# The second expert layer by seven quarter products, with one w2 place in use and a landing place

## The chip, the cores and the metric

The kernel runs on one core of a Trainium2 chip. The metric is device time in microseconds (us) of one execution. TensorE is called PE, VectorE DVE, ScalarE ACT, GpSimd POOL, and SyncE, which only issues transfers here, SP.

## What is computed

A chunked attention gives a row of 512 numbers for each of 4608 tokens. A router picks one of eight experts for each token, and the expert is a layer of two matrices:

```python
logits = xn @ en.T / tau
expert_idx = np.argmax(logits, axis=1)
for e in range(E):
    mask = expert_idx == e
    h = np.maximum(x[mask] @ w1[e], 0.0)          # 512 -> 1024
    out[mask] = gate_w[mask, None] * (h @ w2[e])  # 1024 -> 512
```

All numbers are fp32. The gate is one over the sum of the exponentials of the token's logits.

## The kernel before

A first stage of about 200 us does the attention and the routing, tile by tile, and writes each token's row into a list in memory (`spots`), sorted by expert. A second stage of about 450 us works off this list in steps. A step takes two groups of 64 tokens; group s=0 goes through the experts from the first upwards, group s=1 from the last downwards, so each side s keeps one expert's weights for many steps. The steps are numbered j; the first NE=4 belong to experts 0 and 7 and begin inside the attention, steps 4 to 35 follow (32 steps), and the last ones run under conditions.

The order of instructions is written out by hand: each engine executes its own in the order in which the program states them, and the pools place the waits. The loop at L1141 works in iteration j on hidden layer j+1 and on the result of step j, and prepares step n=j+2.

- **Hidden layer** (`hidden_fast`, L330). x is 128 tokens by 512. Each of the two matrices is cut in quarters (B11, B12, B21, B22), and seven products of sums of quarters replace eight plain ones. Sums of w1 (T1, T2, T4 in `sums_sb`, T3 in the place of B12) are made by `add_up` (L285) when an expert comes; sums of x (s1 to s4) by `add_x` (L309) on DVE in each step. A product is eight matmuls of 32 tokens by 256 columns in four column tiles of PE. ACT copies the first product from PSUM to U, DVE adds the others (`add`, L376) to c11, c12, c22 and U, ACT applies relu (L363, two instructions for each quarter), DVE transposes (L370) into hT. The tile C has four places, for U, c11, c12 and c22, and h two.
- **Result** (`result`, L406). 32 matmuls of 32 tokens by 512 columns over the eight parts of hT, directly with w2, into one of two PSUM banks, in turns. ACT scales with the gate (L423), and one indirect store on POOL (L430) writes whole rows of 512.
- **Weights.** w1 has one place in use and one landing place, `next_w1`. `load_behind` (L188) has SP load the next expert under a condition. `take_next` (L297) is a conditional block on DVE and ACT for each side: where the step begins a new expert, ACT copies three quarters (L303) and DVE makes the four sums (L293). w2 has two whole places per side, which the steps use in turns; `load_w2` (L183) loads each under the condition `fresh`.
- **Gates** (`gate_parts`, L219). POOL raises the sum of squares to the power -1/2 through `halves`, DVE subtracts and scales the logits, ACT takes the exponential with its sum, DVE takes the reciprocal. One gate per partition.
- **Inputs of a step.** `load_x` loads x into one of three places and the logits into `spot`; `turn_xb` (L200) transposes x with DVE. The loop calls them three and two steps ahead.

In the loop of before, in the order of an iteration: the hidden layer j+1 (with the gates, the transposes of x and the sums of x for n in between, `turn_next`, and `take_next` for n after the last product, `swap_next`), then the result of j, then the loads.

Of the kernel before, what the change touches and what calls it, by code (L numbers as in the profile page):

```python
# [25 lines left out]
def kernel(  # L26
# [34 lines left out]
    LONE = NE + 1  # L61

    def buf_of(j):
        return 0 if j < LONE else (j - LONE + 1) % 2

    def next_of(j):

        return j + 1 if j + 1 < LONE else j + 2

# [22 lines left out]
    half = halves[:, 0:1]  # L94
    w1_sb = [keep.tile([P, KD, F], FP32, name=f"w1_{s}") for s in range(2)]
    w2_sb = [[keep.tile([P, KF, D], FP32, name=f"w2_{s}0")] for s in range(2)]
    xin_sb = [keep.tile([P, D], FP32, name=f"xin{i}") for i in range(XBUF)]
    SPOTS = 8
# [8 lines left out]
    fresh = keep.tile([P, NST], I32, name="fresh")  # L107
# [13 lines left out]
    bp = ctx.enter_context(tc.tile_pool(name="blk", bufs=2))  # L121

# [24 lines left out]
    def load_rows(j, rows):  # L147
# [3 lines left out]
        for s in range(2):  # L151
            for b in range(G // Q if s < len(rows) else 0):
                c = s * (G // Q) + b
                ins.append(
                    nc.sync.dma_start(
                        out=xin[j][:, c * P : c * P + P],
                        in_=rows[s][Q * b : Q * b + Q, 0:D].rearrange("i (r d) -> r i d", d=P),
                    )
                )
            ins.append(  # L160
                nc.sync.dma_start(out=spot[G * s : G * s + G, j % SPOTS], in_=rows[s % len(rows)][:, D:RW])
            )
# [20 lines left out]
    def load_w2(j):  # L183
        for s in range(2):
            at = of_step(s, j)
            load_when(w2_sb[s][buf_of(j)], w2_rows, eblk[at], fresh[at])

    def load_behind(j):  # L188

        c = LEAST - 2 - j  # L190
        for s in range(2):
            at = (slice(G * s, G * s + 1), slice(c, c + 1))
            load_when(next_w1[s], w1_rows, after[at], more_e[at])

    def load_late(j):
        for s in range(2 if j != LEAST else 1):
            at = of_step(s, j)
            load_when(next_w1[s], w1_rows, eblk[at], swap[at])

    def turn_xb(j):  # L200
        t = xin.pop(j)
        xT = bp.tile([P, KD, P], FP32, tag="xbT", name="xbT")
# [16 lines left out]
    def gate_parts(j):  # L219
        lg = spot[:, j % SPOTS, 0:E]  # L220
# [3 lines left out]
        last = "_last" if j == LEAST - 1 else ""  # L224
        gate = bp.tile([P, 1], FP32, tag="gate" + last, name="gate", bufs=5)
        nc.gpsimd.tensor_tensor(rn, spot[:, j % SPOTS, SQ : SQ + 1], half, ALU.pow)  # L226
# [12 lines left out]
    def hidden_part(j, s, b, w1, pool, tag, ps=None):  # L239
# [4 lines left out]
        if b == 0:  # L244
# [3 lines left out]
            if s == 0:  # L248
                d["hT"] = bp.tile([P, KF, P], FP32, tag="hT", name="hT", bufs=2)
# [12 lines left out]
        if b == G // Q - 1:  # L262
            h = bp.tile([P, G // Q, KF * Q], FP32, tag="h", name="h", bufs=1)
# [21 lines left out]
    def add_up(s, w1, which):  # L285
        for o, a, b in (
# [3 lines left out]
            ("T4", "T2", "B21"),  # L290
        ):
            if o in which:
                nc.vector.tensor_tensor(  # L293
                    block(s, o), block(s, a, w1), block(s, b, w1), ALU.subtract
                )

    def take_next(j):  # L297

        for s in range(2):
            f = number(swap[of_step(s, j)], 1, ENG.DVE, ENG.Activation)  # L300
            with tc.If(f > 0):  # L301
                for m in ("B11", "B21", "B22"):
                    nc.scalar.copy(block(s, m), block(s, m, next_w1))  # L303
                add_up(s, next_w1, ("T1", "T2", "T3", "T4"))
# [4 lines left out]
    def add_x(j):  # L309

        x = quarters(mo[j]["xT"])
        S = late_p.tile([P, 3, KD // 2, 2, Q], FP32, tag="S", name="S", bufs=2)
        s1, s2, s3, s4 = x[:, 0, 1], S[:, 0], S[:, 1], S[:, 2]
        for o, a, b, op in (
# [5 lines left out]
            nc.vector.tensor_tensor(o, a, b, op)  # L320
        mo[j]["S"] = (s1, s2, s3, s4)

# [7 lines left out]
    def hidden_fast(j, ps_h, gate, turn_next, swap_next):  # L330
# [21 lines left out]


        last = "_last" if j == LEAST - 1 else ""
        hT = bp.tile([P, KF, P], FP32, tag="hT" + last, name="hT", bufs=1 if last else 2)
        d["hT"] = hT
        C = late_p.tile([P, 4, W2], FP32, tag="C", name="C")
        U, c11, c12, c22 = (C[:, i] for i in range(4))
        h = [late_p.tile([P, 2, W2], FP32, tag=f"h{b}", name=f"h{b}") for b in range(2)]

        def relu(b, v, x):
            for s in range(2):
                nc.scalar.activation(  # L363
                    h[b][G * v : G * v + G, s].rearrange("p (k i) -> p k i", i=Q),
# [4 lines left out]
        def turn(b):  # L369
            nc.vector.transpose(  # L370
                hT.rearrange("p k (s b i) -> p b s k i", b=2, i=Q)[:, b],
                h[b].rearrange("p s (k i) -> p s k i", i=Q),
# [8 lines left out]
        next(gate, None)  # L381
        p2 = product(x[:, 1, 0], "B21")
        add(c11, U, p2)
        next(gate, None)
        relu(0, 0, c11)
        turn_next()
        p3 = product(s4, "B22")
        p5 = product(s1, "T1")
        p6 = product(s2, "T2")
        add(U, U, p6)  # L390
        add(c12, U, p5)
        add(c12, c12, p3)
        relu(0, 1, c12)
# [4 lines left out]
        add(c22, U, p5)  # L398
        relu(1, 1, c22)
        p4 = product(x[:, 1, 1], "T4")  # L400
        swap_next()
        add(U, U, p4, ALU.subtract)
        relu(1, 0, U)
        turn(0)
        turn(1)

    def result(j, ps_y):
# [4 lines left out]
        for c in range(KF):  # L412
            for r in range(P // Q):
# [4 lines left out]
                    rhs=w2_sb[s][buf_of(j)][:, c, d0 : d0 + w],  # L418
# [3 lines left out]
        y = bp.tile([P, D], FP32, tag="y", name="y", bufs=1)  # L422
        nc.scalar.activation(y[:, 0:w], ps[:, 0:w], AF.Copy, scale=gate_of.pop(j))  # L423
        to, at, bound = out, spot[:, j % SPOTS, TOK : TOK + 1].bitcast(I32), N - 1
        if one_group:
# [3 lines left out]
            to, at, bound = out.rearrange("n (s d) -> (n s) d", s=2), at2, 2 * N - 1  # L429
        ins = nc.gpsimd.indirect_dma_start(  # L430
            out=to,
            out_offset=bass.IndirectOffsetOnAxis(ap=at, axis=0),
            in_=y[:, 0:w],
# [14 lines left out]
    with (  # L448
# [12 lines left out]
        xr = one.tile([P, NX, W], FP32, name="xr")  # L461
        blank = one.tile([P, W], FP32, name="blank")
        pad(qk_p, 40, "pad_qk")
# [47 lines left out]
        def constant_parts():  # L511
# [46 lines left out]
            nc.gpsimd.tensor_scalar(in_g, second, -float(G), at, ALU.mult, ALU.add)  # L558
            nc.gpsimd.tensor_scalar(e_p, second, float(R), None, ALU.mult)
# [333 lines left out]
        def places(d0, d1):  # L893
# [37 lines left out]
            if d0 == 0:  # L931
                first_e = e_of[:, j1 - 1 : j1]
                nc.vector.tensor_scalar(fresh[:, j1 - 1 : j1], first_e, e_0, None, ne)
                nc.vector.memset(fresh[:, j0 : j1 - 1], 1)
# [4 lines left out]
            else:  # L939
# [4 lines left out]
                    fresh[:, j0:j1], e_of[:, j0:j1], e_of[:, j0 + 2 : j1 + 2], ne  # L944
                )
                nc.vector.tensor_tensor(
# [7 lines left out]
                nc.vector.tensor_tensor(fresh[:, j0:j1], fresh[:, j0:j1], used, ALU.mult)  # L954
# [84 lines left out]
        for t in range(-3, NT + 3):  # L1039
# [31 lines left out]
            if t == NT - 6:  # L1071
                load_first([w[0] for w in w2_sb], w2_rows)
# [38 lines left out]
    pad(late_p, 40, "pad_late")  # L1111
    for s in range(2):
        w2_sb[s].append(late_p.tile([P, KF, D], FP32, name=f"w2_{s}1"))

    next_w1 = [late_p.tile([P, KD, F], FP32, name=f"next_w1_{s}") for s in range(2)]
    sums_sb = [late_p.tile([P, 3, KD // 2, F // 2], FP32, name=f"sums_{s}") for s in range(2)]

    load_x(NE)
    load_x(NE + 1)
    load_w2(LONE)  # L1120

    with (
# [17 lines left out]
        first_parts()  # L1140
        for j in range(LEAST - 1):  # L1141
            n = j + 2

            def turn_next():
                if n < LEAST:
                    turn_xb(n)
                    if n + XBUF < NJ:
                        load_x(n + XBUF)
                    add_x(n)

            def swap_next():
                if NE <= n < LEAST:
# [6 lines left out]
            elif j == 1:  # L1159
                turn_next()  # L1160
                add_up(1, None, TS)
                hidden_plain(2, w1_sb, lambda s: add_up(s, None, ("T3",)))
            else:
                gate = gate_parts(n) if n < LEAST else iter(())
                hidden_fast(j + 1, ps_h, gate, turn_next, swap_next)

            result(j, ps_y)
            if NE <= next_of(j) < NJ:
                load_w2(next_of(j))
            if NE - 1 <= n < LEAST - 1:  # L1170
                load_behind(n)
            elif n == LEAST - 1:
                load_late(LEAST)

        steps = number(n_steps, NST, ENG.PE, ENG.DVE, ENG.Activation, ENG.Pool, ENG.SP)
# [3 lines left out]
        def before_last():  # L1179
            result(LEAST - 1, ps_y)  # L1180
            load_w2(LEAST + 1)

        def step_alone(j, between=None):
            turn_xb(j)
# [4 lines left out]
            if j + 1 < NJ:  # L1189
                load_late(j + 1)  # L1190
# [3 lines left out]
            if j + 2 < NJ:  # L1194
                load_w2(j + 2)
# [51 lines left out]
```

## Time and profile before

| what | value |
|---|---|
| runs | median 673.86 us of 3 (670.34 to 679.64) |
| the profiled execution | 673.45 us, span 671.7 us |
| PE, DVE, ACT, POOL busy | 623.1, 420.9, 353.9, 180.8 us |
| a step without a switch of experts | 12.91 us |
| PE busy from 240 to 600 us | 352 of 360 us |
| expert switches in the loop (copies of L303: 18, three each) | 6 |
| DMA in such a step | 14 to 17% of the engines' time |

How it is read: a row of a group gives line, engine, operation, out<-in, shape and count, then busy time and mean time of one in ns, then how long the engine was idle just before and what ended most of that. In a timeline a row gives start and duration in us, and in brackets the idle time before it. "DVEq" and "ACTq" are the sequencers of the engines: branches, register loads and waits. PE takes an fp32 matmul as two records, and four column tiles run side by side, so the sum of the records' durations is more than PE's busy time.

### The profile page before, as it was taken

To read this page: it belongs to the slowest core of one execution; us is meant where nothing else is said; L and a number is where in the kernel's file an instruction comes from. 1 tells how busy PE (TensorE), PEld (TensorE's weight loads), DVE (VectorE), ACT (ScalarE), POOL (GpSimd) and SP (SyncE) were. 2 spreads that over 40 slices of the span, in tenths; PEclk is the share of its full clock that TensorE was granted. 3 is DMA by queue.
4 is the path that set the end of the run, shared out by engine and by line. 5 is a ranking of instruction groups with operands and counts; after the bars stand their busy time and mean duration, and the time that the engine had idled before them with its cause. 6 is when DMAs were issued, how large, how long until landed. Compare 5 with 4: busy or idle time off the path is not lost. (4 is left out here: it accounts for less than half of the span.)

```text
span 671.7 us, 24786 instructions
## 1 busy us (share of the span) xinstructions
PE 623.1 (93%) x9744; PEld 336.0 (50%) x9744; DVE 420.9 (63%) x1140; ACT 353.9 (53%) x671; POOL 180.8 (27%) x274
## 2 busy tenths in 40 slices
PE   4979988998898989999999999999999999999993
PEld 4868877785443434455334444344444444444431
DVE  2958878885597546547675566757655666565430
ACT  4747766674114444555466546555555566555530
POOL 6739887843330100011000100011001000100101
PEclk9989999998998999999999999999999999999998
DMA  9999999979718711113785111776821115411111
GB/s 248 239 247 253 254 285 274 276 251 368 304 55 297 286 45 34 51 34 129 294 313 181 50 42 42 284 279 238 309 79 57 39 46 170 164 41 35 50 31 35
DMA packets 94686, 112.66 MB, mean 168 GB/s; under 512 B 52460, under 2 KB 72684, under 8 KB 94552
## 3 DMA queue, kind: packets, MB, share of 16 engines
q1 hardware_dynamic: 82824, 72.84, 33.9%
q0 software_dynamic: 11696, 38.04, 17.3%
q8 instruction: 81, 1.33, 0.8%
q14 instruction: 53, 0.43, 0.2%
q10 hardware_dynamic: 32, 0.02, 0.0%
HBM read 334.71 MB, written 22.69 MB: 532 GB/s over the span
## 5 line engine op out<-in xcount | busy, mean ns | idle before, releaser
L415 PE MATMUL y_ps<-w,hT 128*32 128x512 f32 (+1 forms) x2368 | 274.0, 587 | 2.6 <-DVE C L376 2.1
L363 ACT ACTIVATE h<-C 64x256 f32<-64x256 f32 x264 | 179.3, 679 | 108.9 <-DVE C L376 82.4
L415 PEld LDWEIGHTS y_ps<-w,hT 128*32 128x32 f32 x2368 | 85.9, 110 | 161.3 <-issue 146.9
L430 POOL DMA_INDIRECT out_dram<-y,spot x36 | 36.9, 1025 | 412.8 <-ACT C L379 200.1
L376 DVE TENSOR_TENSOR C<-C,h 128x256 f32<-128x256 f32 x231 | 96.1, 416 | 48.3 <-DVEq L301 41.2
L344 PE MATMUL h<-w,S 128*32 128x256 f32 x1056 | 101.4, 382 | 1.8 <-DVE w L293 1.8
L344 PE MATMUL h<-sums,xbT 128*32 128x256 f32 x1056 | 101.0, 383 | 0.0
L344 PE MATMUL h<-w,xbT 128*32 128x256 f32 x1056 | 80.7, 380 | 7.4 <-ACTq L301 5.8
L370 DVE STREAM_TRANSPOSE hT<-h 128x512 f32<-128x512 f32 x66 | 46.7, 708 | 44.7 <-ACT h L363 44.6
L344 PEld LDWEIGHTS h<-w,xbT 128*32 128x32 f32 x1056 | 40.1, 110 | 44.7 <-ACTq L301 14.5
L344 PEld LDWEIGHTS h<-w,S 128*32 128x32 f32 x1056 | 48.0, 110 | 25.4 <-DVE w L293 1.5
L344 PEld LDWEIGHTS h<-sums,xbT 128*32 128x32 f32 x1056 | 48.2, 111 | 22.9 <-issue 0.9
L233 ACT ACTIVATE sh<-sh 128x8 f32<-128x8 f32 x37 | 7.7, 209 | 87.7 <-DVE sh L231 87.7
L229 DVE TENSOR_SCALAR rn<-rn 128x1 f32<-128x1 f32 x37 | 5.7, 153 | 73.3 <-POOL rn L226 73.3
L344 PE MATMUL h<-sums,S 128*32 128x256 f32 x528 | 49.9, 379 | 0.0
L815 POOL DMA_INDIRECT spots<-xr,dest x36 | 37.4, 1038 | 30.6 <-DVE dest L780 10.1
L205 DVE STREAM_TRANSPOSE xbT<-xin 128x256 f32<-128x256 f32 x73 | 44.5, 645 | 0.5 <-DVE hT L370 0.5
L423 ACT ACTIVATE y<-y_ps,gate 128x512 f32<-128x512 f32 (+1 forms) x37 | 25.2, 682 | 29.4 <-issue 13.8
L697 ACT COPY xT<-tr 128x512 f32<-128x512 f32 x36 | 21.1, 586 | 31.3 <-PE tr L695 31.3
L587 POOL DMA_DIRECT2D kx<-in_k_dram x36 | 32.0, 893 | 18.0 <-PE tr L610 17.6
L587 POOL DMA_DIRECT2D qx<-in_q_dram x40 | 34.4, 866 | 1.4 <-PE tr L610 0.7
L695 PE MATMUL tr<-ident,xr 128*128 128x128 f32 x144 | 23.1, 282 | 9.7 <-DVE xr L677 7.2
(200 smaller groups left out, 777.5 us busy)
## 6 DMA issues: line engine op xcount, KB each, us to landing
w<-in_moe_w_dram SPq DMA_DIRECT2D x74, 2048.0 KB
next_w<-in_moe_w_dram SPq DMA_DIRECT2D x67, 2048.0 KB
xin<-spots SPq DMA_DIRECT2D x158, 64.0 KB
qx<-in_q_dram POOLq DMA_DIRECT2D x32, 256.0 KB
v<-in_v_dram SPq DMA_DIRECT2D x56, 144.0 KB
kx<-in_k_dram POOLq DMA_DIRECT2D x28, 256.0 KB
spots<-blank SPq DMA_DIRECT2D x9, 144.0 KB
spot<-spots SPq DMA_DIRECT2D x80, 4.0 KB
```

The lines of the kernel that those rows point to most:

```text
L205: nc.vector.transpose(xT[:, :, cols].rearrange("p c (b i) -> p b c i", i=Q), t[:, s * (D // 2) : (s + 1) * (D // 2)].rearrange("p (b i c) ...
L344: nc.tensor.matmul(ps[t0 : t0 + Q], lhsT=a[:, c, s], rhs=w[:, r], start=c == 0, stop=c == KD // 2 - 1,)
L363: nc.scalar.activation(h[b][G * v : G * v + G, s].rearrange("p (k i) -> p k i", i=Q), x[G * s : G * s + G].rearrange("p (i k) -> p k i", i=Q),
L370: nc.vector.transpose(hT.rearrange("p k (s b i) -> p b s k i", b=2, i=Q)[:, b], h[b].rearrange("p s (k i) -> p s k i", i=Q),)
L376: nc.vector.tensor_tensor(out, a, b, op)
L415: nc.tensor.matmul(ps[Q * r : Q * r + Q, 0:w], lhsT=d["hT"][:, c, Q * t0 : Q * t0 + Q], rhs=w2_sb[s][buf_of(j)][:, c, d0 : d0 + w], start= ...
L423: nc.scalar.activation(y[:, 0:w], ps[:, 0:w], AF.Copy, scale=gate_of.pop(j))
L430: ins = nc.gpsimd.indirect_dma_start(out=to, out_offset=bass.IndirectOffsetOnAxis(ap=at, axis=0), in_=y[:, 0:w], in_offset=None, bounds_ch ...
L587: eng.dma_start(out=x[done : done + n], in_=src[b, :, s : s + n, :].rearrange("h p d -> p h d"),)
L695: nc.tensor.transpose(ps[:, c], d["x"][:, c * P : c * P + P], ident)
L697: nc.scalar.copy(xT, ps)
L815: ins = nc.gpsimd.indirect_dma_start(out=spots, out_offset=bass.IndirectOffsetOnAxis(ap=at, axis=0), in_=m, in_offset=None, bounds_check=S ...
```

## The change

1. `result_fast` takes the place of `result` for steps 4 to 35: w2 and h are cut in quarters, seven products of 16 matmuls with 128 columns each go into seven of eight quarters of two PSUM banks (`ya`, `yb`). ACT copies one product, DVE adds the six others (five instructions of 128 columns, one of 256), ACT scales both halves, and two indirect stores write halves of rows. It is a generator of three parts: products, evacuation, stores. The evacuation of step j-1 runs at the beginning of iteration j, its stores in the middle.
2. A partition of the result now holds half a row of each of two tokens, so two gates are computed per partition (`gates2`), with logits from a second list, `spot2`, that takes four short loads a step instead of two, and `at2` says where the half rows go.
3. w2 has one place in use, `w2_sb`, and a landing place, `next_w2`. `take_next2` is a second conditional block per side at the beginning of an iteration, on ACT (two copies), DVE (three sums) and POOL (one sum, one copy). `load_behind` and `load_late` serve both matrices.
4. The sums of x, and new sums of h (`add_h`, four per step), run on POOL (`add_four`). One sum of w1 (T3) moves to POOL too.
5. Places shrink: C has U and c12 alone, and c11, c12 and c22 follow each other in c12; one h instead of two; one S instead of two. The order of the products in the hidden layer becomes p1, p2, p6, p5, p3, p7, p4.

The core of the diff:

```diff
+    def take_next2(j):
+        for s in range(2):
+            f = number(swap[of_step(s, j)], 1, ENG.DVE, ENG.Activation, ENG.Pool)
+            with tc.If(f > 0):
+                for m in ("B11", "B21"):
+                    nc.scalar.copy(block2(s, m), block2(s, m, next_w2))
+                add_up(s, next_w2, TS, block2)
+                add_up(s, next_w2, ("T3",), block2, nc.gpsimd)
+                nc.gpsimd.tensor_copy(block2(s, "B22"), block2(s, "B22", next_w2))
...
-            nc.vector.tensor_tensor(o, a, b, op)
-        mo[j]["S"] = (s1, s2, s3, s4)
+            nc.gpsimd.tensor_tensor(o, a, b, op)
+        return s1, s2, s3, s4
+
+    def add_x(j):
+        S = late_p.tile([P, 3, KD // 2, 2, Q], FP32, tag="S", name="S")
+        mo[j]["S"] = add_four(quarters(mo[j]["xT"]), S)
+
+    def add_h(j):
+        mo[j]["S2"] = add_four(quarters(mo[j]["hT"]), S2)
...
-        C = late_p.tile([P, 4, W2], FP32, tag="C", name="C")
-        U, c11, c12, c22 = (C[:, i] for i in range(4))
-        h = [late_p.tile([P, 2, W2], FP32, tag=f"h{b}", name=f"h{b}") for b in range(2)]
+        C = late_p.tile([P, 2, W2], FP32, tag="C", name="C")
+        U, c12 = (C[:, i] for i in range(2))
+        h = h_in[-1]
```

The hidden layer's body after the change (`first` is `begin`, below):

```python
        p1 = product(x[:, 0, 0], "B11")
        nc.scalar.copy(U, p1)
        next(gate, None)
        first()
        p2 = product(x[:, 1, 0], "B21")
        add(c12, U, p2)
        relu(0, c12)
        p6 = product(s2, "T2")
        p5 = product(s1, "T1")
        add(U, U, p6)
        add(c12, U, p5)
        turn_next()
        next(gate, None)
        scatter()
        p3 = product(s4, "B22")
        add(c12, c12, p3)
        relu(1, c12)
        for _ in gate:
            pass
        p7 = product(s3, "T3")
        add(U, U, p7)
        p4 = product(x[:, 1, 1], "T4")
        turn(0)
        add(c12, U, p5)
        relu(1, c12)
        add(U, U, p4, ALU.subtract)
        swap_next()
        relu(0, U)
        turn(1)
```

The evacuation and the loop:

```diff
+        nc.scalar.copy(c11, ya[:, 0])
+        add(c21, c11, ya[:, 1])
+        add(c12, c21, yb[:, 2])
+        add(c21, c21, ya[:, 2])
+        add(flat[:, 3 * P :], c21, yb[:, 2])
+        both = flat[:, P : 3 * P].rearrange("p (b w) -> p b w", b=2)
+        add(both, both, yb[:, 0:2])
+        add(c11, c11, yb[:, 3])
+        for b in range(2):
+            nc.scalar.activation(y[:, b], y[:, b], AF.Copy, scale=gate[:, b : b + 1])
...
+            def begin():
+                if NE <= j:
+                    take_next2(j)
+                next(ended, None)
...
+            def scatter():
+                next(ended, None)
+
+            def swap_next():
+                if n < LEAST:
                     add_x(n)
-
-            def swap_next():
                 if NE <= n < LEAST:
                     take_next(n)
...
+            else:
+                ended = result_fast(j, ps_y)
+                next(ended)
+            if by_sevens(j + 1):
+                add_h(j + 1)
```

## The prediction

> **What bounds the kernel now.** I read the page first (busy shares, chain), then busy time in three single steps, then the timelines of each engine in one step, then the waits. The page's chain ends in GpSimd's indirect stores and tells little of the loop, so the step has to be read from the stages.
>
> ```profile
> PE 623.1 (93%) x9744; PEld 336.0 (50%) x9744; DVE 420.9 (63%) x1140; ACT 353.9 (53%) x671; POOL 180.8 (27%) x274
> L363 ACT ACTIVATE h<-C 64x256 f32<-64x256 f32 x264 | 179.3, 679 | 108.9 <-DVE C L376 82.4
> L376 DVE TENSOR_TENSOR C<-C,h 128x256 f32<-128x256 f32 x231 | 96.1, 416 | 48.3 <-DVEq L301 41.2
> ```
>
> Busy time in three steps without an expert switch:
>
> ```profile
> 502.05:514.96 12.91, 12.91 (x184) 5.87 (x179) 7.53 (x23) 7.13 (x13) 1.61 (x2) 1.00 0.17 51
> 514.96:527.87 12.91, 12.91 (x184) 5.78 (x179) 7.70 (x23) 6.68 (x12) 1.60 (x2) 1.00 0.17 52
> ```
>
> Columns are span, PE, weight load, DVE, ACT, POOL: PE works through the whole 12.91 us of a step, DVE 7.5, ACT 6.9, POOL 1.6. PE sets the step. DMA is at 17%.
>
> The timelines of DVE and ACT in one of these steps:
>
> ```profile
> 514.62 0.42 DVE L376 TENSOR_TENSOR C<-C,h 128x256 f32<-128x256 f32 x1 [1.48 <-DVEq L301]
> 517.15 0.71 DVE L370 STREAM_TRANSPOSE hT<-h 128x512 f32<-128x512 f32 x1 [1.49 <-ACT h L363]
> 519.79 0.15 DVE L229 TENSOR_SCALAR rn<-rn 128x1 f32<-128x1 f32 x1 [1.88 <-POOL rn L226]
> 520.71 1.21 DVE L205 STREAM_TRANSPOSE xbT<-xin 128x256 f32<-128x256 f32 x2
> ...
> 515.75 1.37 ACT L363 ACTIVATE h<-C 64x256 f32<-64x256 f32 x2 [0.87 <-ACTq L301]
> 520.51 0.21 ACT L233 ACTIVATE sh<-sh 128x8 f32<-128x8 f32 x1 [2.41 <-DVE sh L231]
> 524.50 2.75 ACT L363 ACTIVATE h<-C 64x256 f32<-64x256 f32 x4 [2.29 <-DVE C L376]
> ```
>
> Read it for slack. DVE's one real pause is 1.88 us: the power on POOL stands behind the store, which waits for the scaled y, which waits for PE. So the DVE and ACT order already takes about 12.91 - 1.9 = 11 us of the 12.91. It is a chain with 1.9 us of slack, though each engine is busy little more than half the time. A pair of conditional blocks costs DVE 1.48 us and ACT 0.87 us even when nothing is switched.
>
> The price of a matmul with 128 moving columns stands in the router's stage, in the same 128x32 tiles:
>
> ```profile
> 56.03 1.08 PE L710 MATMUL rt_ps<-xT,enT 128*32 128x128 f32 x32
> ```
>
> **What the Trainium skill says.** (1) "TensorE: Matmul & The Clock Gate", Back-to-back issue gap: about 81 ns per matmul at N=128 in a stream with weight loads. Here four column tiles share the array: (1.08 - 0.27)/7 is about 0.11 us per four, so the trace decides, against that price. (2) The same title, Architectural detail: only PE reorders, ACT and DVE are strict FIFO. The trace agrees (each row starts after the one before it in the program). (3) "GPSIMD Engine Reference", 3.1 Elementwise: a two-input add over 2048 columns takes 4497 ns on GpSimd, 2293 on DVE. Short POOL rows here (128x41, 302 ns) fit about 0.2 us plus 2.17 ns a column; no longer one is shown. (4) "SBUF — State Buffer", Who interferes with whom: a DVE instruction with two SBUF inputs and a GpSimd instruction that reads SBUF block each other. No run here shows it.
>
> **The change, part by part, against the profiled span of 671.7 us.**
>
> PE. Hidden part: 7 products at 0.86 us = 6.03 in both. The result falls from 12.91 - 6.03 = 6.88 us to 7 products of eight groups of four at 0.11 = 6.2. PE's own step falls to 12.2 us, 0.7 us less; over 31 steps that is 22 us. This is what the change can give, if PE stays the bound.
>
> DVE, ACT: the new order. Four sums of x leave DVE (4 x 0.29 = 1.17). Per step there come: seven-product evacuation (ACT copy 0.27, five DVE adds at 0.29 and one of 256 columns at 0.42, together 1.88, two ACT scalings at 0.47 from the 128x256 row of L423), some 0.55 us of gates in two columns, and a second pair of conditional blocks. By busy time both fit: DVE 7.5 - 1.17 + 1.88 + 0.55 = 8.8, plus 1.48 for blocks; ACT about 7.2, plus 0.9.
>
> What does not fit is the order, because buffers shrink. C has two places instead of four, h one instead of two, and both y banks belong to one step. So c12 = c12 + p5 must wait until ACT has read c11 out of the same place; the third relu pair must wait for the first hT transpose; y's evacuation opens the iteration, and its scalings stand on ACT ahead of the first relu pair. Each wait holds everything behind it: DVE's stalled add holds the x transposes, the gates and the p3 add, for which the next relu waits. DVE and ACT then take turns. One lap, in order:
>
> relu(c21) 1.37; second hT transpose 0.71; DVE's conditional pair for w2 1.48; evacuation adds 1.88; two scalings 0.94; relu(c11) 1.37; add p5 0.42; x transposes 1.21; five gate instructions (0.12 + 0.15 + 0.16 + 2 x 0.19) 0.82; add p3 0.42; relu(c12) 1.37; exp 0.21; four gate instructions 0.59; add p7 0.42, first transpose 0.71, c22 add 0.42; relu(c22) 1.37; ACT's conditional pair for w1 0.87; and again relu(c21). Sum 16.6 us.
>
> Nothing of PE is in this lap: its first product needs only ACT's w1 block, and all 12.2 us of its work fit into 16.6. The conditional pairs of DVE for w1 and of ACT for w2 lie beside the other engine's work, and U's copy and c11's copy beside DVE's transpose. So the step becomes 16.6 us, 3.7 more, over 31 steps 115 us. PE will wait some 4 us a step.
>
> Switches. L303 shows 18 copies, so six switches. Each now puts 3 ACT copies of w1 (1.04 each, 3.1) and, two steps later, 3 DVE sums of w2 (1.22 each, 3.7) into the lap: 6 x 6.8 = 41 us. From 240 to 600 us PE was idle 8 us of 360 before, so +33. The first w2 sums (7.3 us of DVE over two steps) cost about 3 of it.
>
> POOL. Sums of x at 0.47 and of h at 0.75 by price (3), eight a step: 4.9 us. With the power 0.58, two stores 2.05, and two conditional pairs at DVE's 1.48: 10.5 us, under 16.6, so hidden. The power, which stood behind the store, now stands ahead of it and behind the sums of h: 0.7 + 3.3 + 0.6 us after h is turned it is done, and DVE asks for it some 7 us after, so DVE's 1.88 us pause goes and 2.5 us of room stay; without that room a slower POOL goes onto the lap one to one. Below nothing is excluded, since they were never on POOL before; above, at 2.2 times that price POOL sets the lap. The sums of x start when x is transposed, just when DVE's two gate instructions with two SBUF inputs come: by (4) between 0 and 0.9 us a step; I take 0.3, so +9.
>
> SP. Two more short loads a step at about 0.5 us, and w2's conditional loads wait for w2's readers; x is loaded three steps ahead, so this stays hidden (about 1 us a step if it were not). w2 is loaded once per switch instead of for two places: less traffic, and DMA was no bound.
>
> Sum: 115 + 33 + 3 + 9 = +160, span 832. The profiled execution took 673.45 with a span of 671.7, and the median of the runs is 673.86: +2. Time 834.
>
> **The rivals.**
>
> PE stays the bound (ends faster). If DVE and ACT really overlap, as their busy times of 10.3 and 8.1 us would allow, the lap stays under 12.2 us and the step is PE's: 673.9 - 22 = 652. For it: the shares of the page. Against it: the lap has 16.6 us, and it must come below 12.9 for no loss. 3%.
>
> The lap is shorter. DVE instructions without a wait start before the former has ended (in the trace 0.1 us), and register loads hide under waits: a lap of 15 us, 2.1 x 31 = 65, switches 30: about 770. 9%.
>
> POOL becomes the bound. Its sums on strided quarters cost 2.2 to 2.6 times the price, or its conditional blocks are longer; the step goes to 18 to 19 us: 5.5 x 31 + 45, about 890. For it: nothing in the trace shows such sums. Against it: 6 us of room. 14%.
>
> The lap as worked out: 74%.
>
> **How the numbers follow.** 834 is the likeliest. Lap 15.2 to 17.6 with switches between 25 and 45 us gives 780 to 870; the POOL case takes the upper end to 895. Range 780 to 895. A difference over 2% (13 us) is about what a measurement of this kernel can tell. Faster 3%, within 2% 1%, slower 96%.
>
> **What would show it.** In the profile after: steps of about 16.6 us, PE waiting about 4 us in each before the hidden products (for ACT's block or the sums); y7 products with 0.11 us per four; DVE's p5 add and x transposes waiting for ACT's relu; evacuation rows of about 0.29; POOL sums of 0.47 and 0.75 and POOL not released last. Wrong would be: PE at 12.2 a step (the turns overlap), or POOL rows over 1.6 us for the sums of h.

## The result, and the profile after

The kernel after takes 833.12 us (median of four runs, 830.55 to 836.58) where the kernel before, on the same chip, takes 674.76: 1.2348 times, 95% interval 1.225 to 1.2446. Predicted were 834.

The page of the kernel after, first the engines (busy us, share of the span, instructions), then the groups that answer to the two shown of before, with one of PE and one of GpSimd:

```profile
PE 678.1 (82%) x14864; PEld 485.8 (59%) x14864; DVE 488.5 (59%) x1310; ACT 375.4 (45%) x715; POOL 430.5 (52%) x588
...
L409 ACT ACTIVATE h<-C 64x256 f32<-64x256 f32 x264 | 177.2, 671 | 204.6 <-DVE C L422 170.3
L392 PE MATMUL h<-w,xbT 128*32 128x256 f32 x1056 | 125.4, 547 | 87.6 <-ACTq L333 64.6
L361 POOL TENSOR_TENSOR S<-hT 128x256 f32<-128x256 f32 x64 | 53.9, 842 | 202.7 <-DVEq L342 173.0
...
L422 DVE TENSOR_TENSOR C<-C,h 128x256 f32<-128x256 f32 x231 | 95.0, 412 | 52.1 <-ACT h L409 42.7
```

No engine is busy for more than 82% of the span. ACT's relus take 177 us, as before (179), but the idle time ahead of them has grown from 109 to 205 us, and most of it is waiting for DVE's adds. The adds in turn now wait for the relus (42.7 us), which they never did before. DVE's and ACT's instructions did not get slower (an add takes 412 ns in place of 416, a relu 671 in place of 679); they wait for one another. PE's first products (L392, w with x) did get slower, 547 ns in place of 380; the part on the lap below comes back to that.

Busy time in two late steps without a switch (span, PE, weight load, DVE, ACT, POOL, granted clock, DMA share, GB/s):

```profile
608.65:625.60 16.95, 14.59 (x340) 10.23 (x336) 8.34 (x27) 7.05 (x14) 7.44 (x11) 0.90 0.12 34
625.60:642.77 17.17, 14.64 (x340) 10.24 (x336) 8.36 (x27) 7.01 (x14) 7.44 (x11) 0.90 0.13 35
```

A step takes 17 us in place of 12.91. DVE and ACT are busy 8.3 and 7.0 us of it, and the timelines below show how little of that overlaps. (Counted from one copy of U on ACT to the next, steps without a switch take 16.1 to 17.3 us.)

One of these steps on DVE and then on ACT, with the idle time ahead of a row and its releaser in brackets:

```profile
624.98 0.71 DVE L416 STREAM_TRANSPOSE hT<-h 128x512 f32<-128x512 f32 x1 [3.17 <-ACT h L409]
627.48 1.98 DVE L487 TENSOR_TENSOR y<-y,y_ps 128x128 f32<-128x128 f32 x6 [1.79 <-ACT y L489]
...
631.70 0.42 DVE L422 TENSOR_TENSOR C<-C,h 128x256 f32<-128x256 f32 x1 [1.39 <-ACT h L409]
632.03 1.19 DVE L206 STREAM_TRANSPOSE xbT<-xin 128x256 f32<-128x256 f32 x2
...
633.47 0.39 DVE L234 TENSOR_TENSOR sh<-spot,lmax 128x16 f32<-128x16 f32 x1
...
636.25 0.17 DVE L239 TENSOR_REDUCE gates<-sh 128x2 f32<-128x16 f32 x1 [1.68 <-ACT sh L237]
...
642.14 0.71 DVE L416 STREAM_TRANSPOSE hT<-h 128x512 f32<-128x512 f32 x1 [3.41 <-ACT h L409]
```

```profile
625.60 0.37 ACT L425 COPY C<-h 128x256 f32<-128x256 f32 x1 [0.65 <-PE h L392]
627.18 0.27 ACT L489 COPY y<-y_ps 128x128 f32<-128x128 f32 x1 [1.21 <-ACTq L342]
629.49 0.91 ACT L498 ACTIVATE y<-y,gates 128x256 f32<-128x256 f32 x2 [2.05 <-DVE y L487]
630.30 1.36 ACT L409 ACTIVATE h<-C 64x256 f32<-64x256 f32 x2
634.61 1.37 ACT L409 ACTIVATE h<-C 64x256 f32<-64x256 f32 x2 [2.95 <-DVE C L422]
...
640.76 1.35 ACT L409 ACTIVATE h<-C 64x256 f32<-64x256 f32 x2 [1.12 <-ACTq L333]
```

Read the two side by side: while one works the other waits, again and again. The p5 add stands 1.39 us for the relu pair at 630.30, because c11 lies where it must write; the x transposes, the gates and the p3 add stand behind it. The gates' second part stands 1.68 us for the exp, which stands behind the relu pair at 634.61. And the next evacuation begins with ACT's copy at 627.18, which came 1.21 us late, behind ACT's conditional blocks of w2 (line 342); DVE waits 1.79 us for it.

PE in the next step waits for ACT's block of w1:

```profile
639.74 0.63 PE L392 MATMUL h<-w,xbT 128*32 128x256 f32 x4 [2.15 <-ACTq L333]
640.74 3.20 PE L392 MATMUL h<-w,xbT 128*32 128x256 f32 x26 [0.38 <-ACTq L333]
```

### The profile page after: what moved, and what is told of

It is laid out like the page before. It is cut to its first block, busy times and chain, and to the rows that moved or that the text cites. A ratio compares the mean times of both kernels' runs of the same rounds, so it can differ in the third digit from the quotient of the medians.

```text
span 828.8 us, 36864 instructions
## 1 busy us (share of the span) xinstructions
PE 678.1 (82%) x14864; PEld 485.8 (59%) x14864; DVE 488.5 (59%) x1310; ACT 375.4 (45%) x715; POOL 430.5 (52%) x588
## 3 DMA queue, kind: packets, MB, share of 16 engines
q8 instruction: 121, 1.98, 1.0%
## 5 line engine op out<-in xcount | busy, mean ns | idle before, releaser
L392 PE MATMUL h<-w,xbT 128*32 128x256 f32 x1056 | 125.4, 547 | 87.6 <-ACTq L333 64.6
L361 POOL TENSOR_TENSOR S<-hT 128x256 f32<-128x256 f32 x64 | 53.9, 842 | 202.7 <-DVEq L342 173.0
L392 PEld LDWEIGHTS h<-w,xbT 128*32 128x32 f32 x1056 | 47.6, 145 | 150.5 <-ACTq L333 92.1
L422 DVE TENSOR_TENSOR C<-C,h 128x256 f32<-128x256 f32 x231 | 95.0, 412 | 52.1 <-ACT h L409 42.7
L531 POOL DMA_INDIRECT out_dram<-y,at2s x64 | 64.3, 1005 | 65.0 <-POOLq L342 27.6
L392 PE MATMUL h<-sums,xbT 128*32 128x256 f32 x1056 | 97.3, 384 | 0.0
L473 PE MATMUL y_ps<-w,hT 128*32 128x128 f32 x2048 | 87.8, 274 | 10.4 <-DVE y L487 10.4
L473 PE MATMUL y_ps<-sums,hT 128*32 128x128 f32 x2048 | 87.9, 273 | 1.3 <-issue 1.2
L487 DVE TENSOR_TENSOR y<-y,y_ps 128x128 f32<-128x128 f32 (+1 forms) x192 | 56.6, 309 | 49.3 <-ACT y L489 38.5
L473 PE MATMUL y_ps<-w,S 128*32 128x128 f32 x2048 | 76.0, 277 | 5.2 <-POOLq L342 2.6
L392 PE MATMUL h<-w,S 128*32 128x256 f32 x1056 | 76.5, 379 | 0.1
L473 PEld LDWEIGHTS y_ps<-sums,hT 128*32 128x32 f32 x2048 | 70.4, 109 | 1.8 <-issue 1.8
L473 PEld LDWEIGHTS y_ps<-w,S 128*32 128x32 f32 x2048 | 63.8, 111 | 9.3 <-POOLq L342 4.6
L392 PE MATMUL h<-sums,S 128*32 128x256 f32 x528 | 63.6, 473 | 0.4 <-POOL S L361 0.4
L392 PEld LDWEIGHTS h<-sums,xbT 128*32 128x32 f32 x1056 | 49.1, 114 | 23.9 <-issue 0.8
L392 PEld LDWEIGHTS h<-w,S 128*32 128x32 f32 x1056 | 40.6, 110 | 23.5 <-DVE w L327 0.6
L473 PE MATMUL y_ps<-sums,S 128*32 128x128 f32 x1024 | 44.1, 277 | 3.5 <-POOL S L361 3.5
```

The costliest lines, as they stand in the source:

```text
L361: nc.gpsimd.tensor_tensor(o, a, b, op)
L392: nc.tensor.matmul(ps[t0 : t0 + Q], lhsT=a[:, c, s], rhs=w[:, r], start=c == 0, stop=c == KD // 2 - 1,)
L422: nc.vector.tensor_tensor(out, a, b, op)
L473: nc.tensor.matmul(o[t0 : t0 + Q], lhsT=a[:, c, s], rhs=block2(s, m)[:, c, r], start=c == 0, stop=c == KF // 2 - 1,)
L487: nc.vector.tensor_tensor(out, a, b, ALU.add)
L531: ins = nc.gpsimd.indirect_dma_start(out=to, out_offset=bass.IndirectOffsetOnAxis(ap=at, axis=0), in_=y, in_offset=None, bounds_check=boun ...
```

## Experiments

Kernels named together ran on one chip with their own runs of the kernel before (median 674 to 683 us), so the ratios to before are compared: the kernel after stands at 1.2348. Start times of steps are those of the second layer's products in each trace.

One thing bears on all these comparisons. In the kernel after, ACT's copy of U waits 12.3 us for PE in all, for a reason given below ("The lap"), and PE's mean granted clock is 0.911. In two_places, x_sums_dve, no_w2_switch, exp_first, gate_in_relu, pool_more and one_flag the copy waits only 1 to 3 us in all, and the clock is 0.94 to 0.97. So about 10 us of each gain "by the ratio" in these runs, an estimate from these waits, are not the work of the edit, and a loss is that much larger than it looks.

**Do the shared places cost the time, or PE, or GpSimd?** Four kernels. The first gives h and c11 places of their own again:

```
-        h = h_in[-1]
+        h = h_in[-1], xin_sb[2].rearrange("p (b f) -> p b f", b=2)
+        c11 = h[1][:, 0]
...
-        add(c12, U, p2)
-        relu(0, c12)
+        add(c11, U, p2)
+        relu(0, 0, c11)
...
-        relu(1, c12)
+        relu(1, 1, c12)
```

> The kernel after, with one thing undone: the second expert layer's h has two places again (the third place of x is given up for it, x is loaded two steps ahead), c11 of the first hidden quarter lies in the second h place and c22 in c12's, so neither the p5 add nor the third relu pair waits for a reader of the same place. Theory (DVE and ACT take turns and their lap sets the step): relu(c11), 1.37 us, now runs beside the p5 add and the x transposes instead of ahead of them, and the third relu pair no longer stands behind the first transpose; 1.4 to 2 us a step go, 31 steps, so 770 to 790 us. Rival PE (half-speed stretches and 128-column products bound the step): no change, 833. Rival POOL (its sums bound it): no change, 833.

Measured: 798.0 us, 1.1724 (1.1615 to 1.1833). By the ratio 42 us went; steps without a switch fell to 14.8 to 15.5. That is the theory's side, at its lower end of 43 us, and below it without the 10 us named above. The p5 add (the second of the two adds at 599.96) no longer waits:

```profile
599.45 0.41 DVE L423 TENSOR_TENSOR xin<-C,h 128x256 f32<-128x256 f32 x1
599.96 0.94 DVE L423 TENSOR_TENSOR C<-C,h 128x256 f32<-128x256 f32 x2
600.83 1.21 DVE L206 STREAM_TRANSPOSE xbT<-xin 128x256 f32<-128x256 f32 x2
```

The second leaves out half of PE's second layer:

```
-            for c in range(KF // 2):
+            for c in range(1):
```

> The kernel after with half of the second layer's products left out: each of the seven takes one of its two row blocks of w2, so the rows written are not the layer's. PE's own work falls by half of 6.7 us a step. Theory (lap of DVE and ACT): no change, 825 to 840; PE idles 3.3 us more in each step, and its granted clock falls further. Rival PE: 31 steps x 3.3 us less, about 730.

Measured: 846.07 us, 1.2443 (1.2346 to 1.2541), the same as after within the intervals. One of its steps:

```profile
648.00:665.00 17.00, 11.45 (x171) 5.92 (x168) 8.20 (x27) 7.00 (x13) 7.38 (x11) 0.80 0.12 34
```

PE has half the second layer's matmuls and the step still takes 17.00 us. PE's second layer is no bound. PE waits the more: its granted clock falls to 0.822, and U's copy now waits for PE in nearly every step, 18.5 us in all in place of 12.3.

The third puts the sums of x back on DVE (`eng.tensor_tensor`, with nc.vector for x).

> The kernel after with the four sums of x back on DVE (at the same place in the order), those of h stay on GpSimd: GpSimd loses 1.9 us a step, DVE gains four of about 0.29, 1.2 us. Theory (lap): in this place they lie behind the c21 add, while ACT works through the fourth relu pair and its conditional block, so most is hidden: 825 to 850. Rival POOL: its work sets the step, so up to 1.9 us x 31 less, 775 to 800. Rival PE: 833.

Measured: 840.37 us, 1.2368 (1.227 to 1.2467). The total is unchanged, as the theory had it, but it hides two movements: steps without a switch take 16.0 us, hardly less than those steps of after in which U's copy does not wait (16.1 to 16.6), and switch steps take up to 24.6, where after has at most 21.9. GpSimd as the bound would have shown in every step.

```profile
616.00:632.00 16.00, 13.94 (x336) 10.17 (x336) 8.98 (x30) 7.02 (x14) 5.60 (x7) 1.00 0.13 39
```

The fourth is the kernel before with only the hidden part's shrunk places and their order:

```
-        C = late_p.tile([P, 4, W2], FP32, tag="C", name="C")
-        U, c11, c12, c22 = (C[:, i] for i in range(4))
-        h = [late_p.tile([P, 2, W2], FP32, tag=f"h{b}", name=f"h{b}") for b in range(2)]
...
+        C = late_p.tile([P, 2, W2], FP32, tag="C", name="C")
+        U, c12 = (C[:, i] for i in range(2))
+        h = late_p.tile([P, 2, W2], FP32, tag="h0", name="h0")
...
```

The products go from p1, p2, p3, p5, p6, p7, p4 to p1, p2, p6, p5, p3, p7, p4, and the first transpose of h comes ahead of c22.

> The kernel before, and of the change only the hidden part's shrunk places with the order that belongs to them (C of two quarters, one h, products in the order p1 p2 p6 p5 p3 p7 p4); the plain second layer, w2 in two places and all sums on DVE stay. Theory (lap): p5 add waits for relu(c11) and so on; one lap is c11 add 0.42, relu 1.37, p5 add 0.42, x transposes 1.21, x sums 1.17, gates 0.6, p3 add 0.42, relu 1.37, exp 0.21, gates 0.3, p7 add, transpose and c22 add 1.55, relu 1.37, ACT's conditional pair 0.87, relu 1.37, transpose 0.71, y's scaling 0.9: 14.3 us against PE's 12.9, so 31 x 1.4 = 43 us, about 717. Rival (places cost nothing, the loss is the second layer's additions): 674, no change. Rival PE: 674.

Measured: 731.17 us, 1.077 (1.0683 to 1.0856); steps of 14.4 us against the 14.3 worked out. Some 32 steps with 1.5 us more than 12.9 make the 48 us. So a third of the loss comes with the shrunk places and their order, before any seven-product second layer exists.

**Which rows stand in the lap?** Four kernels. Without the conditional blocks of w2 (`for s in range(0)` in take_next2):

> The kernel after without the conditional blocks of w2 (its weights are still loaded, but the first two experts' w2 serves all seven-product steps, so the rows of later experts are not theirs). Theory: DVE's pair of blocks (1.48 us) leaves the lap of every step, and with it ACT's, which delays U's copy and c11's copy (0.5 us in the profile after); less some 0.3 us since the evacuation then waits for PE's last result; 1.2 to 2 us a step, 37 to 62 us, and in six switches three DVE sums each, 22 us: 1.2348 times before falls to about 1.13 (750 to 775 us where before takes 675). Rival (the blocks lie beside other work, only switching costs): 22 us, 1.20. Rival PE: 1.235.

Measured: 771.24 us, 1.1293 (1.1207 to 1.138); steps without a switch 14.5 to 15.0. As expected. DVE now evacuates as soon as it has transposed:

```profile
604.11 0.71 DVE L416 STREAM_TRANSPOSE hT<-h 128x512 f32<-128x512 f32 x1 [3.21 <-ACT h L409]
604.74 1.94 DVE L487 TENSOR_TENSOR y<-y,y_ps 128x128 f32<-128x128 f32 x6
```

By the ratio 71 us went, some 60 of them with the edit. A step without a switch is 1.4 us shorter than one of after in which U's copy does not wait, and 26 of the 32 steps switch no w2: that is some 37 us. So the tests that switch nothing cost in all at least as much as the switches of w2.

The exp ahead of the relu pair:

```
         add(c12, c12, p3)
+        next(gate, None)
         relu(1, c12)
```

> The kernel after with one line moved: the gates' exp is issued to ACT ahead of the relu pair of c12, not behind it. Nothing is added or left out. Theory: DVE's second gate part, and the p7 add, the first transpose and the c22 add behind it, wait for exp only, not for relu(c12) first; but the transpose needs relu(c12) itself. Out of the lap go the four gate instructions 0.59 and the p7 add 0.42 less the 0.1 to 0.2 that exp now costs ahead of the relu: 0.8 to 1.1 us a step, 25 to 34 us, about 1.19 times before. Rival PE or POOL: 1.235.

Measured: 797.0 us, 1.1704 (1.1618 to 1.179), 43 us by the ratio where 25 to 34 were expected; the surplus is about the 10 us of missing waits named above. DVE's rows in one step:

```profile
628.86 0.41 DVE L422 TENSOR_TENSOR C<-C,h 128x256 f32<-128x256 f32 x1
629.22 0.17 DVE L239 TENSOR_REDUCE gates<-sh 128x2 f32<-128x16 f32 x1
...
630.72 0.71 DVE L416 STREAM_TRANSPOSE hT<-h 128x512 f32<-128x512 f32 x1 [0.28 <-ACT h L409]
```

The 1.68 us ahead of L239 are gone and 0.28 ahead of the transpose took their place. A moved line, with no work taken away, gives some 4% back.

The gate's factor in the relus:

```
                     AF.Relu,
+                    scale=gate_of[j][0][G * s : G * s + G, v : v + 1] if by_sevens(j) else 1.0,
...
-        for b in range(2):
-            nc.scalar.activation(y[:, b], y[:, b], AF.Copy, scale=gate[:, b : b + 1])
```

(In c12 and c21 the factor taken is that of the other half of the tokens, so these rows are not the layer's; the work is the same.)

> The kernel after with the gate's factor put into the relus of the hidden part (relu with a factor per row; the gate is positive, and the two layers are linear behind it), so the two scalings of y on ACT are gone. Theory: they stand on ACT ahead of relu(c11) in the lap: 2 x 0.5 us a step and the handover between DVE's last evacuation add and ACT, 31 x 0.9 to 1.1, 28 to 34 us: about 1.19 times before. Rival PE or POOL, or that scalings lie beside DVE's work: 1.235.

Measured: 837.36 us, 1.2298 (1.2209 to 1.2388): a miss, no gain. The group of the relus says why:

```profile
L409 ACT ACTIVATE h<-C,gates 64x256 f32<-64x256 f32 x256 | 195.4, 763 | 284.6 <-DVE C L423 237.0 <-ACTq L333 23.4 <-DVE sh L235 16.3
```

A relu with a factor per row takes 763 ns, not 671; eight a step are 0.74 us more in the lap. Against that, only about half of the two scalings had stood in it: in the kernel after the first relu starts 0.84 us behind the last evacuation add (630.30 against 629.46), and here it starts 0.36 us behind it, when DVE's add to c11 is done:

```profile
616.20 1.98 DVE L488 TENSOR_TENSOR y<-y,y_ps 128x128 f32<-128x128 f32 x6 [1.32 <-ACT y L490]
618.54 1.56 ACT L409 ACTIVATE h<-C,gates 64x256 f32<-64x256 f32 x2 [2.52 <-DVE C L423]
```

So 0.48 us of scalings went and 0.74 us of relu came.

More work on GpSimd:

```
-        mo[j]["S2"] = add_four(quarters(mo[j]["hT"]), S2)
+        x = quarters(mo[j]["hT"])
+        for _ in range(4):
+            nc.gpsimd.tensor_tensor(S2[:, 1], x[:, 0, 0], x[:, 0, 1], ALU.subtract)
+        mo[j]["S2"] = add_four(x, S2)
```

> The kernel after with four further sums of h on GpSimd ahead of the four (written to a place that is then overwritten): GpSimd gets 3 us more work a step. Theory: GpSimd has some 2.5 us of room before the power is wanted, so 0 to 1 us a step, and some of it through sums that block DVE: 1.235 to 1.28 times before. Rival POOL: 3 us x 31 = 93 us one to one, 1.37. Rival PE: 1.235.

Measured: 852.84 us, 1.2508 (1.2418 to 1.2598), by the ratio about 11 us more than after (some 20 with the missing waits) for some 100 us of work added. An ordinary step:

```profile
282.00:298.30 16.30, 13.83 (x344) 11.78 (x336) 8.03 (x26) 7.04 (x14) 10.40 (x15) 1.00 0.13 34
```

GpSimd carries 10.4 us there and the step does not grow. GpSimd is no bound in such a step. What was lost lies in the steps around a switch, which take up to 25.3 us from copy to copy of U where after has at most 23.9.

**Can the lap be shortened below PE's step?** Three kernels, then one. One flag ahead of each pair of blocks (for w1 and for w2; the sums of the flags, `any_f`, are made once beforehand):

```
+        g = number(any_f[of_step(0, j)], 2, ENG.DVE, ENG.Activation, ENG.Pool)
+        with tc.If(g > 0):
             for s in range(2):
                 f = number(swap[of_step(s, j)], 1, ...)
                 with tc.If(f > 0):
```

> The kernel after with one flag a step ahead of each pair of conditional blocks (the sum of the two groups' flags, worked out once beforehand): where nothing is switched, an engine loads and tests one number for a pair, not two. Theory: what of a pair lies in the lap is halved, DVE's for w2 1.48 to about 0.8, ACT's for w1 0.87 to about 0.45, ACT's for w2 likewise; in some 25 steps without a switch 1.0 to 1.4 us less, in a switch step up to 0.8 more: 20 to 35 us less, 1.18 to 1.205 times before. Rival (blocks lie beside other work) and rival PE: 1.235.

Measured: 798.43 us, 1.1758 (1.1671 to 1.1846), 40 us by the ratio where 20 to 35 were expected, some 30 without the missing waits. Steps without a switch took 14.5 to 15.0. ACT's wait behind its blocks of w1 fell from between 0.87 and 1.12 us to 0.20, and that ahead of the evacuation's copy from 1.21 to 0.60.

Two edits together, two_places and exp_first:

> Two h places (as in two_places) and the exp ahead of the relu pair of c12 (as in exp_first) together. Theory: the first takes 1.5 to 2 us, the second about 1.5 us out of different parts of one lap, so they add up as long as DVE's and ACT's lap stays over PE's step of 12.2 to 12.9: 1.2348 - 0.062 - 0.064 = 1.108 times before, 1.10 to 1.13. Rival (both shorten the same wait): 1.15 to 1.17.

Measured: 768.92 us, 1.1322 (1.1241 to 1.1402); steps 14.0 to 14.3. Of the 0.127 that the two would give if they added up, 0.103 came, at the edge of the theory's 1.13 and short of its 1.108. The missing 0.024, 16 us, need not be an overlap of the two: U's copy waits 11.7 us for PE here, and 1.6 and 2.0 in the two kernels alone.

All of them together, with w2's blocks moved behind the first relu pair and w1's third copy moved to GpSimd:

> All that shortened the lap, together: two h places, exp ahead of the relu pair of c12, one flag for a pair of blocks, w2's blocks behind the first relu pair in place of ahead of the evacuation, and w1's third copy at a switch on GpSimd in place of ACT. Theory: steps without a switch come down to PE's own 12.2 to 12.9 us and PE waits for nothing there, so the clock stays up; switches still cost 4 to 8 us each and the first w2 sums about 10: 1.02 to 1.07 times before, and still over the kernel before. If PE's second layer really gains 0.7 us a step and the switches are hidden: 0.98. If another wait stands behind the lap: 1.10.

Measured: 757.63 us, 1.1125 (1.1043 to 1.1207): outside the 1.02 to 1.07 expected. Steps without a switch fell only to 13.3 to 13.9, and the rest is switching: from the first step at 270.5 us to the one at 718.8 us there are 29 steps in 448 us; at 13.6 they would be 394, so the six switches cost some 54 us, 9 each.

In these steps PE sets the pace again:

```profile
588.97:602.35 13.38, 12.91 (x343) 11.97 (x339) 8.43 (x27) 7.01 (x13) 7.06 (x12) 1.00 0.16 45
```

```profile
597.48 0.37 ACT L430 COPY C<-h 128x256 f32<-128x256 f32 x1 [1.41 <-PE h L396]
```

PE is busy 12.91 of 13.38 us at a clock of 1.00 and waits for no other engine from 584 to 603 us, while ACT waits for it, 43.9 us in all at U's copy. PE's step is not the 12.2 us of the prediction: the hidden part takes about 6 us and the second layer 7.4 to 8.6, with pauses like those shown next. So here another wait stood behind the lap, and it was PE's. This kernel is the shortest version found with the second layer in sevens, and still 11% over the kernel before.

In the kernel with two places and the early exp, PE itself pauses in the second layer where no wait is shown (start, us, then idle ahead and releaser in brackets):

```profile
610.15 0.75 PE L475 MATMUL y_ps<-w,S 128*32 128x128 f32 x4
611.34 0.32 PE L475 MATMUL y_ps<-w,S 128*32 128x128 f32 x2 [0.44 <-issue]
612.10 1.69 PE L475 MATMUL y_ps<-w,S 128*32 128x128 f32 x52 [0.44 <-issue]
```

Six records of matmuls start in 1.95 us, then 52 take 1.69. The layer takes 8.4 us a step in place of 6.7. It is no matter of these two edits: in steps without a switch it takes 7.4 us and more in every run on these three chips that has the second layer in sevens whole, x_sums_dve and pool_more included. The next loads of x and the indirect stores start there, so the stores were moved, in a run on a fourth chip:

```
-        scatter()          # behind the x transposes
...
                     add_x(n)
+                scatter()
```

> The kernel of places_and_exp with one line moved: the two indirect stores are issued behind the sums of x, some 2.5 us later in GpSimd's order, so they no longer start together with the next loads of x. Open after the runs so far: where DVE and ACT no longer hold the step, PE's second layer takes about 8.4 us in place of 6.7, with a pause of some 1.9 us in it in which four matmuls start per 0.75 us and no wait is shown; it lies where x's loads and the indirect stores begin. If the stores bring it, the pause moves 2 to 3 us later with them or goes; if the loads of x bring it, it stays about 1.2 us behind the first load; if PE's own stream of instructions brings it, neither place nor size changes with the transfers. The lap of DVE and ACT is not touched: 1.12 to 1.14 times before, down to 1.10 if the pause goes.

Measured: 760.3 us, 1.1263 (1.1201 to 1.1324), the same within the intervals. The same products in this kernel:

```profile
602.29 1.66 PE L474 MATMUL y_ps<-w,S 128*32 128x128 f32 x52
```

The pause is gone and the layer takes 6.7 us again, but the step stays at 14.0 to 14.3: PE now waits for ACT's block instead, 0.75 and 0.31 us ahead of its products in the step at 607 us. The pause had filled slack. Whether it went with the stores' place is not shown: the chip changed with it, and in the kernel after, where stores and loads start together too, PE does not pause either. The kernel before took 674 to 675 us beside these two, and 682 to 683 us on each of the three chips where PE pauses. So the chip is as good a suspect as the stores.

## Why the prediction was right, and where its terms were off

**The bound.** The likeliest case was that DVE and ACT take turns and their lap, not an engine's busy time, sets the step. The experiments show it from three sides: taking away half of PE's second layer (half_result) or adding 3 us of GpSimd work a step (pool_more) changes little, while each edit that takes a wait or a block out of the turns, without touching PE's work, gives 40 to 71 us by the ratio, some 30 to 60 by itself (two_places, exp_first, one_flag, no_w2_switch).

**The lap.** 16.6 us were worked out, 16.9 with the read lock. Measured from copy to copy of U, in steps without a switch: 16.1 to 16.6 where that copy waits 0.4 us or less for PE, 16.9 to 17.3 where it waits 0.6 or more. The wait comes from PE's clock, which the prediction did not foresee. In the step shown PE, after waiting, soon runs at half rate:

```profile
622.70:624.40 1.70, 1.46 (x12) 0.54 (x16) 0.00 (x0) 0.82 (x3) 0.00 (x0) 0.76 0.00 0
624.40:626.10 1.70, 1.70 (x20) 0.79 (x16) 0.71 (x1) 0.92 (x2) 0.26 (x1) 0.50 0.00 0
```

The clock falls to 0.50, and ACT's copy of U, which the prediction had beside DVE's transpose, waits 0.65 us for the first product. In the step at 289 us the clock was 1.00 ahead of the copy, and the copy came with no wait. In half_result, where PE waits more, the clock ahead of the copy is 0.50 and the wait about 0.65 us in nearly every step. The Trainium skill, "TensorE: Matmul & The Clock Gate", Part 1: The HAM clock gate, says that the array falls to half rate after an idle window of about 3.4 us and returns after a busy one. The trace agrees in kind (0.50 behind PE's waits, mean clock down from 0.985 to 0.911) but not in size: PE's longest idle time ahead of this is 2.23 us, and the measurement decides. "Nothing of PE is in this lap" is thus the step of the prediction that failed: PE's wait makes its first product slower, and that product then lengthens the lap, 12.3 us in all.

**The step "The conditional pairs ... of ACT for w2 lie beside the other engine's work, and U's copy and c11's copy beside DVE's transpose" failed too.** ACT's blocks of w2 stand between the two copies (1.22 us), and DVE's evacuation waits for the second copy even where U's copy comes with no wait:

```profile
289.39 0.37 ACT L425 COPY C<-h 128x256 f32<-128x256 f32 x1
290.98 0.27 ACT L489 COPY y<-y_ps 128x128 f32<-128x128 f32 x1 [1.22 <-ACTq L342]
```

```profile
291.42 1.98 DVE L487 TENSOR_TENSOR y<-y,y_ps 128x128 f32<-128x128 f32 x6 [1.32 <-ACT y L489]
```

So ACT's copies and blocks stand in the lap, and DVE's own pair of blocks lies beside them. Over the run DVE's evacuation waits 38.5 us for ACT's copy and 3.8 for its own sequencer. In size this cost nothing here: 2.06 us from the relu's end to the evacuation, where the sum has 2.19 (transpose 0.71 and DVE's pair 1.48). With U's copy waiting for PE it is 2.53.

**Luck.** That the sum came within 1 us of the measured time is in part luck. A step without the wait for PE is about 0.5 us shorter than the 16.9 worked out, some 17 us over 31 steps; DVE's rows start about 0.1 us before the former has ended, as the rival of the shorter lap had it. The waits for PE add 12 us and the switches 5 more than their 41. These nearly cancel. The mechanism and the range do not rest on that.

**Terms by size.** PE's second layer: 6.2 worked out, 6.7 measured from its first start to its last end, so that of the 0.7 us a step that PE could gain some 0.2 is left (12.91 less 6.03 and 6.7). Sums on GpSimd: 0.47 and 0.75 worked out; measured 0.46 to 0.49 for x, 0.81 to 0.84 for h. (The 2.17 ns a column behind these two is nearer 2.1 by the figures given beside it, which moves them by less than 0.02.) Scalings 0.47: measured 0.50, of which half stands in the lap. Evacuation 1.88: measured 1.98 (six adds in a row). The relu as taken; ACT's blocks of w1 0.87 to 1.12 where 0.87 was taken. The read lock: the Trainium skill, "SBUF — State Buffer", Who interferes with whom, says that a DVE instruction with two SBUF inputs and a GpSimd instruction that reads SBUF contend. It was counted at 0.3 us a step with no run to show it. Now the trace agrees: the two gate instructions of L234 and L235 took 0.30 and 0.27 us on average (0.39 and 0.35 in the step shown), with GpSimd's sums of x starting beside them, and 0.17 and 0.18 in the kernel with two places, where these sums start 2 us later. In x_sums_dve, where the sums of x are not on GpSimd, they took 0.15 and 0.17 outside the switch steps. That is 0.2 us a step, within the 0 to 0.9 that were kept.

**The switches.** 6.8 us each were worked out. From the step at 260.7 us to the one at 790.5 us there are 29 steps in 529.8 us; at a mean of 16.7 they would be 484, so 46 us for six, 7.6 each, with three DVE sums and three ACT copies in a row in each. That is the second reason why no order found comes back to the kernel before: w1's copies and sums lay beside PE's work before (PE was idle 8 us of 360 in all) and have no cover now, and those of w2 are new.

**The rivals.** "PE stays the bound" (652 us) fell with half_result. "GpSimd becomes the bound" (890 us) fell with pool_more. "A shorter lap" (770 us) had steps of 15 us: by the starts of U's copy no step of after from 220 us on came under 16.1.

**What stays open.** PE's pauses in the second layer, with chip and place of the stores as suspects; and how long PE must wait for its clock to fall. The 10 us taken off the gains are an estimate from the waits, as the kernel after has no trace on the other chips.

## What to carry to other kernels

When a change shrinks buffers, write the two engines' queues side by side and add up the rows along the turns: busy shares of 59% and 45% hid a chain that was full. Before adding blocks that are seldom taken, price what they cost when not taken, on each engine, in every step: here, for w2, that was at least as much as the work they guarded. And look for instructions that stand behind a long one in their queue without needing it, as the exp did: moving it took no work away and cost nothing.

## What the runs showed of the hardware

- ACT's relu of 64x256 takes 671 ns with no factor and 763 ns with a factor read per row.
- Conditional blocks that are not taken cost time on each engine that tests. A pair held DVE 1.48 us in the kernel before, and ACT 0.87 to 1.12 us ahead of a relu and 1.21 ahead of a copy in the kernel after; with one flag for the pair ACT's two waits were 0.20 and 0.60.
- PE's granted clock fell to 0.50 behind idle times of 2.2 us in steps of 17 us.
- GpSimd's power over 128x2 values takes 0.82 us in the kernel after, 0.72 in pool_more.
- PE can lose most of 1.9 us in a stretch of 128-column matmuls without any wait for another engine that the profile shows, at a granted clock of 1.00, six records starting in that time. It did so on three chips and not in the two runs with whole products beside a kernel before of 674 to 675 us; the cause is open.
